# Block-sparse attention and a gated feed-forward: all heads visited whole, values in float32 by query half

## The chip, the cores and the metric

The kernel runs on one core of a Trainium2 chip. Its engines are TensorE (PE; PEld is its weight load), VectorE (DVE), ScalarE (ACT), GpSimd (POOL) and SyncE (SP), which issues most of the DMAs. The metric is the time of one execution on the device in microseconds (us), lower is better. Inputs and output lie in DRAM.

## The reference

There are 4 batches, 8 heads, 768 positions, head size 64, and blocks of 32 positions. The feed-forward has width 512 inside 2048.

```python
scores = scale * np.matmul(q, k.transpose(0, 1, 3, 2))      # per batch and head
mask = neighbours | first/last block row or column | 3 sampled blocks per block row
scores = np.where(mask, scores, -1000000000.0)
attn = softmax(scores)                                      # exp(scores - max) / (sum + 1e-9)
x = concat over heads of attn @ v                           # (4*768, 512)
h = x @ w_in
g = np.where(h >= 1, h, np.where(h <= -1, 0.0, (h + 1) ** 2 / 4))
out = g @ w_out
```

The mask is known only at run time, so the whole 768 x 768 score matrix is computed. The weights `moe_w_in` and `moe_w_out` arrive as 64-bit floats, which the kernel reads as pairs of 32-bit words and converts itself.

## The kernel before

**Numbers.** TensorE takes two kinds of operands here. A "rounded" one (fp32r) goes through in one record of a matmul; a float32 one in two. Where float32 accuracy is kept with rounded operands, a number is split into a rounded high part and the rounded rest, and two or three matmuls are added: scores are [q;k] high plus the cross terms (lines 411 and 412), the gated layers three products each (588 to 590, 624 to 626).

**A visit** (function `visit`) handles one head, or half of its queries. The queries and keys lie as columns (768 of them, in six tiles of 128, two halves of 384). Steps of a visit:

1. Maxima: 128 x 384 score tiles with the mask added through extra rows of q and k (line 356), reduced on VectorE (362), transposed on TensorE (375 or 379) and written with a minus sign into one more row of q (ScalarE, 384 or 387, or VectorE, 390).
2. Scores, transposed: keys on 128 partitions, 384 queries (409, or 411 and 412); the row of maxima takes part, so that ScalarE's exponential (416) follows at once.
3. Values: v times exponentials, accumulated over six key tiles (`values`).
4. Row sums of the exponentials, their reciprocal, and the product (x). For two heads at a time this makes 128 rows of x, which are split in high and rest (519, 524).

Before the change there are four forms. Batch 0 is visited twice: visits 0 to 7 take the first query half of each head with float32 scores straight from the loaded tiles (409); visits 8 to 15 the second half with split scores. Both multiply values in float32 at full width (445): v's 64 columns and 64 columns of ones, so that the row sums come out of the same matmul. Batch 1 (visits 16 to 23) multiplies values in float32 in two column groups of 64: even key tiles go to partitions 0 to 63 of the result, odd ones to 64 to 127 (448), and the two are added (457, 463). Batches 2 and 3 split the exponentials (ScalarE's cast, VectorE's subtraction at 424) and v, and take two rounded matmuls for each tile (451, 452). Outside batch 0, GpSimd adds the exponentials up (433), VectorE reduces them (479) and a small matmul finishes the row sums (485).

**The gated layers** (function `moe`) run for one half of a batch's rows at a time: 16 steps `fi` over the 2048 inner columns, each with 12 matmuls of 384 columns into `hp`, the gate on ScalarE and VectorE, and 9 matmuls of 512 columns into three accumulators `oa0` to `oa2`. Batch b's layers stand beside the attention of batch b+1; after the last batch they stand alone.

**Conversions** of the weights (`convert`) run on ScalarE and VectorE: one absolute value, four steps of 1024 columns (187 to 193) and two splits of 512 (200) for each of 8 pieces of w_in and 8 of w_out. The converted w_out is kept in DRAM and read again by each pass.

**What sets the order.** Every step is put in a list with a due time (`at(t, fn, ...)`, in units of one score tile, from tables of numbers at the end of the file) and emitted in that order; the scheduler of the tile framework then orders each engine's instructions by its own model of when operands are ready. Each engine executes its own order strictly. Score tiles share banks of PSUM: `pa` (three), and in batch 0 a ring of `oa0`, `oa1` and `hp` for the scores.

## Time and profile before

| What | us |
|---|---|
| Runs | 986.56, 989.36, 990.48 (median 989.36) |
| Profiled execution | 989.12 |
| Its span, first to last instruction | 987.3 |
| TensorE busy | 954.8 |
| VectorE busy | 691.8 |
| ScalarE busy | 636.5 |
| First scores | at 23.9 |
| First half of batch 0 | 23.9 to 98.2 |
| Second half of batch 0, with the start of the first gated pass | 98.2 to 205 |
| Batch 1, with the rest of batch 0's gated passes | 205 to 403 |
| Batches 2 and 3 | 403 to 845 |
| Gated passes alone | 845 to 987 |

How to read the profile: an engine's busy time is the union of its instructions' times. Matmuls overlap in their pipeline, so a matmul's own duration is longer than the time until the next one starts; the timeline by start times tells the rate. A float32 matmul appears as two records. Rows of the timeline give start, duration, engine, line, operation, output<-input and form, and in brackets the idle time before it with what ended it.

### The profile page before, as it was taken

The numbers are of one execution on the slowest core, as the hardware profiler recorded it, in microseconds if no ns is written. First come the engines' busy times: TensorE is split into PE (matmuls) and PEld (weight loads), VectorE is DVE, ScalarE is ACT, GpSimd is POOL, SyncE is SP. The second block draws the span as 40 slices with busy tenths as digits, with TensorE's granted clock in tenths as the row PEclk, the third lists the DMA queues.
The fourth block names the chain that finished last, engine by engine and source line by source line (L and its number), as shares of the span: only waits on it lengthen the run. The fifth ranks groups of instructions, "written<-read, shape, count | busy, mean of one in ns | idle before, by whom it ended". The sixth has DMA issues, their size and how long they took to land.

```text
span 987.3 us, 14438 instructions
## 1 busy us (share of the span) xinstructions
PE 954.8 (97%) x4770; PEld 811.0 (82%) x4770; DVE 691.8 (70%) x1268; ACT 636.5 (64%) x1286; POOL 263.1 (27%) x252
## 2 busy tenths in 40 slices
PE   2999999999999999999999999999999999999998
PEld 1656687877778777799999989999989999899997
DVE  3899976778756576888888897888888885422222
ACT  3698887665555554777767676767767676533433
POOL 1000000036444444333433343343433334000000
PEclk9999999999999999999999999999999999999999
DMA  6456764644555554655455444655545342433432
GB/s 181 135 183 221 216 200 159 180 138 136 153 168 152 143 154 133 178 155 171 140 142 176 139 137 144 185 158 153 157 132 168 115 126 86 155 128 128 160 128 96
DMA packets 55102, 150.83 MB, mean 153 GB/s; under 512 B 9414, under 2 KB 20310, under 8 KB 54004
## 3 DMA queue, kind: packets, MB, share of 16 engines
q1 hardware_dynamic: 54836, 149.42, 50.1%
q8 instruction: 38, 0.62, 0.3%
q10 hardware_dynamic: 192, 0.49, 0.1%
q14 instruction: 36, 0.29, 0.1%
HBM read 106.77 MB, written 14.80 MB: 123 GB/s over the span
## 4 chain that ended last, share of the span: by engine, by line
PE 86%; DMA 4%; ACT 4%; DVE 3%; issue 2%; SPq 0%; POOL 0%; ACTq 0%; DVEq 0%; POOLq 0%
PE oa L624 9%; PE oa L626 8%; PE oa L625 8%; PE hp L588 8%; PE hp L590 7%; PE hp L589 7%; PE pa L356 6%; PE pa L411 5%; PE pa L412 5%; PE po L445 4%; PE po L451 4%; PE po L452 3%; PE po L448 3%; PE oa L409 2%; PE oa L445 1%
## 5 line engine op out<-in xcount | busy, mean ns | idle before, releaser
L362 DVE TENSOR_REDUCE mc<-pa 128x1 f32<-128x384 f32 x384 | 204.9, 548 | 37.1 <-PE pa L356 34.0
L433 POOL TENSOR_TENSOR acc<-acc,pt 128x384 f32<-128x384 f32 x144 | 156.1, 1084 | 206.3 <-ACT pt L416 171.9
L416 ACT ACTIVATE pt<-pa 128x384 f32<-128x384 f32 x272 | 132.9, 489 | 59.0 <-PE pa L412 51.4
L588 PE MATMUL hp<-x,wi 128*128 128x384 f32 x448 | 156.7, 350 | 0.5 <-DVE r L603 0.5
L624 PE MATMUL oa<-w,gh 128*128 128x512 f32 x384 | 156.2, 407 | 0.3 <-ACT gh L215 0.3
L626 PE MATMUL oa<-w,gl 128*128 128x512 f32 x384 | 151.5, 394 | 0.0
L589 PE MATMUL hp<-x,wi 128*128 128x384 f32 x448 | 151.4, 338 | 0.0
L590 PE MATMUL hp<-x,wi 128*128 128x384 f32 x448 | 151.3, 338 | 0.0
L625 PE MATMUL oa<-w,gh 128*128 128x512 f32 x384 | 150.9, 393 | 0.0
L356 PE MATMUL pa<-KA,QA 88*128 88x384 f32 x384 | 143.0, 389 | 7.7 <-ACT QA L215 4.6
L424 DVE TENSOR_TENSOR pl<-pt,ph 128x384 fp32r<-128x384 f32 x192 | 125.7, 655 | 29.1 <-ACT ph L215 28.5
L215 ACT CAST ph<-pt 128x384 fp32r<-128x384 f32 x192 | 98.8, 515 | 69.8 <-PE po L451 66.9
L603 DVE SCALAR_TENSOR_TENSOR r<-r,hp 128x384 f32<-128x384 f32 x112 | 61.5, 549 | 86.0 <-ACT r L599 85.3
L411 PE MATMUL pa<-QA,KA 102*128 102x384 f32 (+1 forms) x336 | 116.3, 346 | 0.0
L412 PE MATMUL pa<-QB,KB 128*128 128x384 f32 x336 | 114.1, 340 | 0.0
L356 PEld LDWEIGHTS pa<-KA,QA 88*128 88x128 f32 x384 | 73.2, 192 | 34.8 <-DVE mc L362 7.4
L595 ACT ACTIVATE r<-hp,half_c 128x384 f32<-128x384 f32 x112 | 65.1, 582 | 52.8 <-PE hp L590 50.6
L614 DVE TENSOR_TENSOR gl<-r,gh 128x384 fp32r<-128x384 f32 x128 | 74.3, 580 | 27.4 <-ACT gh L215 26.8
L588 PEld LDWEIGHTS hp<-x,wi 128*128 128x128 f32 x448 | 84.5, 189 | 8.1 <-issue 1.8
L215 ACT CAST gh<-r 128x384 fp32r<-128x384 f32 x128 | 65.6, 513 | 32.8 <-DVE r L603 32.2
L589 PEld LDWEIGHTS hp<-x,wi 128*128 128x128 f32 x448 | 84.4, 188 | 2.6
L626 PEld LDWEIGHTS oa<-w,gl 128*128 128x128 f32 x384 | 72.1, 188 | 17.2
(125 smaller groups left out, 1676.1 us busy)
## 6 DMA issues: line engine op xcount, KB each, us to landing
w<-wo_dram SPq DMA_DIRECT2D x112, 512.0 KB
qk<-in_qk_t_dram SPq DMA_DIRECT2D x24, 384.0 KB
raw<-in_moe_w_in_dram SPq DMA_DIRECT2D x8, 1024.0 KB
raw<-in_moe_w_out_dram SPq DMA_DIRECT2D x16, 512.0 KB
wo_dram<-w SPq DMA_DIRECT2D x16, 512.0 KB
lv<-in_v_dram SPq DMA_DIRECT2D x40, 192.0 KB
den<-s SPq DMA_DIRECT2D x64, 96.0 KB
out_dram<-o SPq DMA_DIRECT2D x7, 768.0 KB
```

The source lines that it names most:

```text
L215: eng.copy(out=dst, in_=src)
L356: nc.tensor.matmul(out=pm[:, 0:HALF], lhsT=QAi[0:KM, t * 128:(t + 1) * 128], rhs=KAi[0:KM, kh * HALF:(kh + 1) * HALF], start=True, stop=True)
L362: nc.vector.reduce_max(out=st["mc"][:, t - t0, kh:kh + 1], in_=st.pop(("pm", t, kh))[:, 0:HALF], axis=AX.X)
L411: nc.tensor.matmul(out=ps[:, 0:HALF], lhsT=KAi[0:k, ks], rhs=QAi[0:k, cs], start=True, stop=False)
L412: nc.tensor.matmul(out=ps[:, 0:HALF], lhsT=st["KB"][:, ks], rhs=st["QB"][:, cs], start=False, stop=True)
L433: nc.gpsimd.tensor_tensor(out=st["acc", hf], in0=prev, in1=st["p", hf, c], op=ALU.add)
L588: nc.tensor.matmul(out=hv, lhsT=wi[:, j, 0, fs], rhs=x[:, 0], start=(j == 0), stop=False)
L589: nc.tensor.matmul(out=hv, lhsT=wi[:, j, 0, fs], rhs=x[:, 1], start=False, stop=False)
L590: nc.tensor.matmul(out=hv, lhsT=wi[:, j, 1, fs], rhs=x[:, 0], start=False, stop=(j == NP - 1))
L624: nc.tensor.matmul(out=o, lhsT=gh[:, ts], rhs=w[:, 0], start=(fi == 0), stop=False)
L625: nc.tensor.matmul(out=o, lhsT=gh[:, ts], rhs=w[:, 1], start=False, stop=False)
L626: nc.tensor.matmul(out=o, lhsT=gl[:, ts], rhs=w[:, 0], start=False, stop=(fi == NF - 1))
```

## The change

All 32 heads are visited once, whole, in one form. q and k are loaded together (768 columns), rounded on ScalarE, and copied to their places by DMA; the scores are always two rounded matmuls (now lines 323 and 324). Values are always float32 in two column groups of 64, but the groups now are the two query halves (345): all 12 matmuls of a head belong to one step, and the results are copied without an addition (352). v needs no split and no ones any more, the exponentials aren't split. Maxima are always transposed to one row, six transposes a head (302).

In batch 0 the row sums come from TensorE: 12 float32 matmuls a head with a stationary tile of 32 columns of ones, dealt out to four column groups of 32 (368). The sums go through DRAM to be turned (377, 383). In the other batches GpSimd adds the exponentials up as before, for the two halves one after the other, and the reduction and the finishing matmul are done once for a pair of heads instead of once for each half.

Batch 0's gated passes now begin after batch 0's attention. They are split by `fi`: first half 0 with steps 0 to 7, then half 1 with all 16, then half 0 with steps 8 to 15. The partial output of the first goes to DRAM and is read back and added in the third (537). Conversions are cut so that each piece serves one quarter of w_in's columns for two row tiles, and the tables of due times are new.

Core of the diff:

```diff
+    def mask_half(hf, eng):
+        cs = slice(hf * HALF, (hf + 1) * HALF)
+        pm = psa.tile([128, 512], F32, name="pa")
+        nc.tensor.matmul(out=pm[0:NB, 0:HALF], lhsT=early["mb"][M], rhs=KAt[0][64:KM, cs], start=True, stop=True)
+        rounded(eng, QA[0][64:KM, cs], pm[0:NB, 0:HALF])
...
+    def visit(n, b, h, pst):
 
         j, e = divmod(h, 2)
+        n0 = PER * n
         wide = n < H
-        raw = n in RAW
-        whole = n in WHOLE
-        tiled = n in TILED
-        row = n in ROW
-        G = {**P, **PW} if wide else {**P, **PX} if n < 2 * H else {**P, **PA} if n < 3 * H else P
-        o0, o1 = (L, R) if e == 0 else (R, L)
+        G = {**P, **PW} if wide else {**P, **PA} if n < 2 * H else P
+        o0 = (L, R)[e]
         QAi, KAi = QA[n % SETS], KAt[n % SETS]
...
+        at(-99 if n == 0 else n0 - G["qs"] - G["ld"], load_qk)
+        at(n0 - G["qs"] - 0.4, hi)
+        at(n0 - G["qs"] + 0.2, hi_one)
+        at(n0 - G["qs"] + 0.4, lo)
+        at(n0 - G["qs"] + 1.3, hi_two)
+        at(n0 - G["qs"] + 1.6, lo_two)
...
-            ps = st["ps", c] = bank(wide)
-            k = 97 if row else KA
-            if raw:
-                nc.tensor.matmul(out=ps[:, 0:HALF], lhsT=KF[n % RAWS][0:k, ks], rhs=QF[n % RAWS][0:k], start=True, stop=True)
-                return
-            nc.tensor.matmul(out=ps[:, 0:HALF], lhsT=KAi[0:k, ks], rhs=QAi[0:k, cs], start=True, stop=False)
+            ps = st["ps", hf, c] = bank(wide)
+            nc.tensor.matmul(out=ps[:, 0:HALF], lhsT=KAi[0:97, ks], rhs=QAi[0:97, cs], start=True, stop=False)
...
-        def p_hi(hf, c):
-            ph = st["ph", c] = pp.tile([128, HALF], F32R, name="ph")
-            rounded(nc.scalar, ph, st["p", hf, c])
-
-        def p_lo(hf, c):
-            pl = st["pl", c] = pp.tile([128, HALF], F32R, name="pl")
-            nc.vector.tensor_tensor(out=pl, in0=st["p", hf, c], in1=f(st["ph", c]), op=ALU.subtract)
+            p = st["p", hf, c] = pp.tile([128, HALF], F32, name="pt")
+            nc.scalar.activation(out=p, in_=st.pop(("ps", hf, c))[:, 0:HALF], func=AF.Exp, scale=SCALE)
...
-            if whole:
-                nc.tensor.matmul(out=po, lhsT=st["vn"][:, c], rhs=st["p", hf, c], start=(c == 0), stop=(c == T - 1))
-                return
-            if tiled:
-                nc.tensor.matmul(out=st["po", hf][R if c % 2 else L, 0:HALF], lhsT=st["lv"][:, c], rhs=st["p", hf, c],
-                                 start=(c < 2), stop=(c >= T - 2))
-                return
-            nc.tensor.matmul(out=po, lhsT=st["vn"][:, c], rhs=st["ph", c], start=(c == 0), stop=False)
-            nc.tensor.matmul(out=po, lhsT=st["vn"][:, c], rhs=st["pl", c], start=False, stop=(c == T - 1))
...
+        def values(g):
+            after(("V", n, g), *[("V", n, k) for k in range(g)])
+            if g == 0:
+                st["po"] = psc.tile([128, DM], F32, name="oa2") if wide and n % 2 else pso.tile([128, 512], F32, name="po")
+            for c in range(g * VG, (g + 1) * VG):
+                for hf in range(2):
+                    nc.tensor.matmul(out=st["po"][(L, R)[hf], 0:HALF], lhsT=st["lv"][:, c], rhs=st["p", hf, c],
+                                     start=(c == 0), stop=(c == T - 1))
+
+        def o_copy(hf):
+            after(("x", b, j, hf, e), ("V", n, T // VG - 1))
+            if e == 0 and hf == 0:
+                pst["xun"] = pr.tile([128, 2, HALF], F32, name="xun", bufs=2)
+            nc.scalar.copy(out=pst["xun"][o0, hf], in_=st["po"][(L, R)[hf], 0:HALF])
...
+        def p_tot():
+            after(("tot", n), ("V", n, T // VG - 1))
+            pd = st["tot"] = bank(wide)
+            for c in range(T):
+                for hf in range(2):
+                    k = 2 * (c % 2) + hf
+                    nc.tensor.matmul(out=pd[k * 32:(k + 1) * 32, 0:HALF], lhsT=ones, rhs=st["p", hf, c],
+                                     start=(c < 2), stop=(c >= T - 2))
+
+        def p_row():
+            after(("ps", b, j, e), ("tot", n))
             if e == 0:
...
+                pst["s1"] = dr.tile([2, 2, 2, HALF], F32, name="s1", bufs=2)
+            a = ac.tile([128, 2, HALF], F32, name="acc")[:, 0]
+            nc.scalar.copy(out=a, in_=st["tot"][:, 0:HALF])
+            Q_S1.dma_start(out=pst["s1"][e].rearrange("q f c -> (q f) c"), in_=a[0:128:32])
+
+        def r_in():
+            after(("in", b, j), ("ps", b, j, 0), ("ps", b, j, 1))
+            t = pst["rt"] = pr.tile([48, 2, 32], F32, name="rt")
+            for k in range(2):
+                Q_T.dma_start(out=t[k * 24:(k + 1) * 24], in_=pst["s1"][k].rearrange("q f (a j) -> (f a) q j", j=32))
+
+        def r_den():
+            after(("r", b, j), ("in", b, j))
+            t = pst["r"] = pr.tile([48, 32], F32, name="rc", bufs=2)
+            nc.vector.scalar_tensor_tensor(out=t, in0=pst["rt"][:, 0], scalar=1e-9, in1=pst["rt"][:, 1], op0=ALU.add, op1=ALU.add)
...
+        if wide:
+            at(u + 0.01, p_tot)
+            at(u + G["al"], p_row)
             if e:
...
+        def o_tile():
+            g["out"] = op.tile([128, 3, DM], F32, name="o")
+            if not first:
+                after(("back", b, hf), ("part", b, hf))
+                Q_OUT.dma_start(out=g["out"], in_=part)
+
         def o_copy(t):
-            after(("oc", b, hf, t), *[("l2", b, hf, k, t) for k in range(NF)])
-            if t == 0:
-                g["out"] = op.tile([128, 3, DM], F32, name="o")
-            if end and t == 1:
...
+    full = tuple(range(NF))
+    low, high = full[:NF // 2], full[NF // 2:]
+    t = PER * H + D0
+    for hf, fis, new in ((0, low, low), (1, full, high), (0, high, ())):
+        moe(t, STEP0, 0, hf, fis, new)
+        t += STEP0 * len(fis)
+    for k in range(2, 2 * B):
+        moe(PER * H * (1 + k / 2) + DELAY, PER * H / 2 / NF, k // 2, k % 2, full)
...
-RAW = tuple(range(8))
-WHOLE = tuple(range(16))
-TILED = tuple(range(16, 24))
-LV, VG, VD = 3, 6, 0.0
-ROW = tuple(range(24))
-KMOVE = 0
...
+LV, PT, VG, XT = 3, 14, 6, 10
+STEP0 = 2.598
+D0 = 10.127
```

How the order moves, at the places that the prediction uses. TensorE in batch 0, in a visit's second part, before (409 float32 scores, 356 maxima of the next visit, 445 values at full width):

```order
L409 MATMUL oa_521<-QB,KB 128x384
L356 MATMUL pa<-KA_116,QA_114 128x384
L445 MATMUL oa_509<-pl,vn 128x384
L409 MATMUL oa_531<-QB,KB 128x384
L356 MATMUL pa<-KA_116,QA_114 128x384 x2
L445 MATMUL oa_509<-pt,vn 128x384
L409 MATMUL hp<-QB,KB 128x384
```

The same place now (323 and 324 scores, 285 maxima of the next head, 345 values in column groups, 368 row sums, 302 transposes):

```order
L345 MATMUL oa_1172<-pt,lv 64x384 x2
L285 MATMUL pa<-KA_112,QA_110 128x384 x2
L323 MATMUL oa_1152<-QA_111,KA_113 128x384
L285 MATMUL pa<-KA_112,QA_110 128x384
L324 MATMUL oa_1152<-QB,KB 128x384
L345 MATMUL oa_1172<-pt,lv 64x384 x2
L285 MATMUL pa<-KA_112,QA_110 128x384 x2
L345 MATMUL oa_1172<-pt,lv 64x384 x2
L285 MATMUL pa<-KA_112,QA_110 128x384
L345 MATMUL oa_1172<-pt,lv 64x384
L368 MATMUL oa_1185<-pt,ones 32x384 x9
L302 MATMUL pa<-idr,mr 1x128 x6
```

Single float32 matmuls at full width among the maxima have become short groups of one or two matmuls in column groups, and a block of row sums stands ahead of the transposes. Over batch 0 the 96 value matmuls (345) stand in 56 such groups and the 96 row-sum matmuls (368) in 25.

TensorE in the later batches, before (451 and 452 values, 624 to 626 the second gated layer, 411 scores):

```order
L626 MATMUL oa_5785<-w,gl 128x512
L451 MATMUL po<-ph,vn 128x384
L452 MATMUL po<-pl,vn 128x384
L624 MATMUL oa_5803<-w,gh 128x512
L625 MATMUL oa_5803<-w,gh 128x512
L626 MATMUL oa_5803<-w,gl 128x512
L411 MATMUL pa<-QA_114,KA_116 128x384
```

And now (523 gated layer, 393 finishing matmul of the row sums, 345 values, 323 and 324 scores, 487 gated layer):

```order
L523 MATMUL oa_6587<-w,gl 128x512
L393 MATMUL pa<-sel,PS_114 64x32
L345 MATMUL po<-pt,lv 64x384 x12
L323 MATMUL pa<-QA_111,KA_113 128x384
L324 MATMUL pa<-QB,KB 128x384
L487 MATMUL hp<-x,wi 128x384
```

Twelve pairs of rounded value matmuls, spread over a head, have become one closed group of twelve.

VectorE at the start, before (362 reductions of the first maxima, 188 and 189 conversion of w_in, 367 the maxima's last step):

```order
L362 TENSOR_REDUCE mc<-pa 128x1 x6
L188 TENSOR_SCALAR cva<-cva 128x1024
L367 TENSOR_TENSOR mr<-mc 128x3
L189 TENSOR_SCALAR cva<-cva 128x1024
L362 TENSOR_REDUCE mc<-pa 128x1 x2
```

And now (258 the rest of q and k, 220 the mask's row, 291 reductions, 296 the maxima's last step, 197 conversion):

```order
L258 TENSOR_TENSOR qk<-qk,qkh 128x768
L220 CAST QA_110<-pa 24x384
L291 TENSOR_REDUCE mc<-pa 128x1 x12
L296 TENSOR_TENSOR mr<-mc 128x6
L197 TENSOR_SCALAR cva<-cva 128x1024
```

The first conversion step has moved behind the first head's maxima, which are twelve instead of six.

More of the change, by code (lines that the diff above doesn't have):

```diff
@@ L394, in visit, with max_turn @@
-        jobs = [(t, kh) for t in tiles for kh in range(2)]
+            nc.vector.tensor_tensor(out=mr, in0=st["mc"][:, :, 0], in1=st["mc"][:, :, 1], op=ALU.max)
+        def max_turn(hf):
+            after(("turn", n, hf), ("col", n))
+            pm = st["pr", hf] = bank(wide, "m")
+            for t in range(TH):
+                nc.tensor.transpose(out=pm[0:1, t * 128:(t + 1) * 128].bitcast(F32R),
+                                    in_=st["mr"][:, hf * TH + t:hf * TH + t + 1], identity=idr)
@@ new lines, in sums, with dens, recip @@
+        def sums():
+            after(("sums", b, j), ("ps", b, j, 0), ("ps", b, j, 1))
+            pd = st["pd"] = bank(wide)
+            nc.tensor.matmul(out=pd[0:64, 0:32], lhsT=pst["ps"], rhs=sel, start=True, stop=True)
+        def dens():
+            after(("r", b, j), ("sums", b, j))
+            t = pst["r"] = pr.tile([48, 32], F32, name="rc", bufs=2)
+            nc.vector.tensor_single_scalar(out=t, in_=st["pd"][0:48, 0:32], scalar=1e-9, op=ALU.add)
+        def recip():
+            after(("rr", b, j), ("r", b, j))
+            nc.vector.reciprocal(out=pst["r"], in_=pst["r"])
+            pst["den"] = pr.tile([128, S], F32, name="den", bufs=1)
+            s2 = dr.tile([2, S], F32, name="s2", bufs=2)
+            Q_S2.dma_start(out=s2.rearrange("e (a b) -> (e a) b", b=32), in_=pst["r"])
+            for k in range(2):
+                Q_DEN.dma_start(out=pst["den"][k * 64:(k + 1) * 64], in_=s2[k:k + 1].to_broadcast([64, S]))
@@ L523, in x_lo @@
             x = xt[b, j, hf]
[L524 to L528 removed]
+            nc.vector.tensor_tensor(out=x[:, 1], in0=pst["xun"][:, hf], in1=f(x[:, 0]), op=ALU.subtract)
+        for c in range(T):
+            for hf in range(2):
+                s = n0 + 2 * c + hf
                 at(s, scores, hf, c)
                 at(s + G["ex"], expo, hf, c)
[L531 to L534 removed]
+                if not wide:
@@ new lines, in visit @@
+        for hf in range(2):
+            at(u + G["ot"], o_copy, hf)
+        if wide:
+            at(u + 0.01, p_tot)
+            at(u + G["al"], p_row)
+            if e:
+                y = u + G["su"]
+                at(y, r_in)
+                at(y + G["de"], r_den)
+        else:
+            at(n0 + 2 * T - 1 + G["al"] + G["ps"], acc_sum)
+        if e and not wide:
+            y = u + G["su"] + (PER if h < H - 1 else G["al"])
+            at(y, sums)
+            at(y + G["de"], dens)
@@ L562, in body, with moe @@
+        if e:
+            at(y + G["re"], recip)
+            y += G["r2"] + G["re"]
+            at(y + G["xm"], x_mul)
+            for hf in range(2):
+                at(y + G["xh"] + 0.01 * hf, x_hi, hf)
+                at(y + G["xl"] + 0.01 * hf, x_lo, hf)
     wo_dram = dr.tile([NF, 128, 2 * DM], F32R, name="wo_dram")
-    def moe(t0, p, b, hf, first):
+    part = dr.tile([128, 3, DM], F32, name="part")
+    def moe(t0, p, b, hf, fis, new=()):
         g = {}
-        G = {**P, **PM} if first else P
+        G = {**P, **PM} if new else P
+        first, final = fis[0] == 0, fis[-1] == NF - 1
```

438 lines of the change are left out of this document (126 added, 312 removed).

## The prediction

> **What bounds the kernel now.** I read part 1 of the page first, then the stages by windows, then the order in time of TensorE alone.
>
> ```profile
> PE 954.8 (97%) x4770; PEld 811.0 (82%) x4770; DVE 691.8 (70%) x1268; ACT 636.5 (64%) x1286; POOL 263.1 (27%) x252
> 23.90:98.20 74.30, 73.72 (x252) 45.20 (x251) 67.21 (x114) 61.19 (x119) 0.00 (x0) 1.00 0.56 179
> 98.20:205.00 106.80, 104.21 (x476) 81.03 (x475) 85.78 (x147) 83.33 (x164) 1.25 (x1) 1.00 0.63 191
> 205.00:403.00 198.00, 193.69 (x1021) 151.07 (x1019) 130.01 (x236) 112.10 (x229) 87.78 (x81) 1.00 0.50 146
> 403.00:624.00 221.00, 219.92 (x1160) 203.56 (x1161) 184.78 (x348) 156.96 (x328) 85.06 (x80) 1.00 0.52 152
> 624.00:845.00 221.00, 220.11 (x1161) 203.37 (x1161) 177.37 (x334) 156.05 (x328) 84.30 (x79) 1.00 0.48 141
> 845.00:987.30 142.30, 138.09 (x693) 123.93 (x691) 39.41 (x72) 57.99 (x109) 0.00 (x0) 1.00 0.39 133
> ```
>
> A window row gives length, then busy time of PE, PEld, DVE, ACT, POOL, granted clock, DMA share and GB/s. TensorE fills every stage after the first scores; the others have room. So I count what TensorE has to issue. A busy matmul overlaps its neighbour, so a price is the distance from one start to the next:
>
> ```profile
> 318.21 0.34 PE L411 MATMUL pa<-QA,KA 97*128 97x384 f32 x1
> 318.39 0.34 PE L412 MATMUL pa<-QB,KB 128*128 128x384 f32 x1
> 318.56 0.33 PE L588 MATMUL hp<-x,wi 128*128 128x384 f32 x1
> ...
> 319.09 0.52 PE L375 MATMUL pa<-idr,mr 128*1 128x128 f32 x6
> 319.45 0.39 PE L588 MATMUL hp<-x,wi 128*128 128x384 f32 x1
> ...
> 321.43 0.39 PE L624 MATMUL oa<-w,gh 128*128 128x512 f32 x1
> 321.66 0.40 PE L625 MATMUL oa<-w,gh 128*128 128x512 f32 x1
> ```
>
> A rounded (fp32r) matmul of 384 columns costs 0.175 us, one of 512 columns 0.233, a transpose of a maximum 0.36/6 = 0.06. Float32 at full width:
>
> ```profile
> 36.86 0.81 PE L445 MATMUL po<-pt,vn 128*128 128x384 f32 x2
> 37.50 0.81 PE L409 MATMUL hp<-QB,KB 97*128 97x384 f32 x2
> 37.85 0.81 PE L356 MATMUL pa<-KA,QA 88*128 88x384 f32 x2
> 38.50 0.81 PE L445 MATMUL po<-ph,vn 128*128 128x384 f32 x2
> ```
>
> One float32 matmul is two records. From 36.86 to 38.50 lie one value matmul, one float32 score and two maxima: (1.64 - 0.35)/2 = 0.645 each, with nothing lost at the changes. Float32 in column groups, first a closed group of six, then scattered:
>
> ```profile
> 313.11 0.33 PE L356 MATMUL pa<-KA,QA 88*128 88x384 f32 x1
> 313.38 0.54 PE L448 MATMUL po<-pt,lv 128*64 128x384 f32 x1
> 313.38 0.54 PE L448 MATMUL po<-ph,lv 128*64 128x384 f32 x1
> 313.75 0.49 PE L448 MATMUL po<-pt,lv 128*64 128x384 f32 x1
> ...
> 314.07 0.49 PE L448 MATMUL po<-pl,lv 128*64 128x384 f32 x1
> ...
> 315.46 0.44 PE L356 MATMUL pa<-KA,QA 88*128 88x384 f32 x1
> 315.74 0.40 PE L624 MATMUL oa<-w,gh 128*128 128x512 f32 x1
> ```
> ```profile
> 217.54 0.33 PE L356 MATMUL pa<-KA,QA 88*128 88x384 f32 x1
> 217.81 0.54 PE L448 MATMUL po<-pt,lv 128*64 128x384 f32 x1
> 217.82 0.54 PE L448 MATMUL po<-ph,lv 128*64 128x384 f32 x1
> 218.60 0.44 PE L356 MATMUL pa<-KA,QA 88*128 88x384 f32 x1
> 218.98 0.86 PE L448 MATMUL po<-pl,lv 128*64 128x384 f32 x2
> 219.77 0.44 PE L356 MATMUL pa<-KA,QA 88*128 88x384 f32 x1
> ```
>
> The two groups start together, and a record follows every 0.32 us: a pair of matmuls costs one slot of 0.64. But the group of three slots takes 313.11 to 315.74, less two rounded matmuls of 0.175: 2.28, where 3 x 0.64 = 1.92. So each **run** (column-group matmuls with none at full width between) pays 0.36 for getting in and out. A lone matmul with no partner (218.60 to 219.77, less one maximum) costs 0.99: as much as a pair, and 1.5 times the full-width 0.645. This is what the change multiplies.
>
> I check the prices on the kernel before. Batch 0, first half: 96 float32 (61.9), 48 maxima (8.4), 24 transposes (1.4) = 71.7 of the 74.3. From 98.2 to 403: 48 float32 (31.0), 816 rounded of 384 (142.8), 279 of 512 (65.0), 16 runs (36.5), 72 transposes (4.3) = 280 of 304.8. From 403 on: 2112 of 384 (369.6), 873 of 512 (203.4), 16 transposes (1) = 574 of 584.3. So 3, 25 and 10 us are waits and the tail.
>
> **The change part by part.** Counts are from TensorE's order in the changed program.
>
> Start: before, the first scores wait for a conversion that stands among VectorE's first maxima:
>
> ```profile
> 13.97 2.88 DVE L362 TENSOR_REDUCE mc<-pa 128x1 f32<-128x384 f32 x6 [2.81 <-PE pa L356]
> 20.26 1.12 ACT L187 ACTIVATE cva<-raw 128x1024 f32<-128x1024 f32 x1 [4.80 <-DMA raw<-in_moe_w_in_dram]
> 22.03 0.15 DVE L367 TENSOR_TENSOR mr<-mc 128x3 fp32r<-128x3 f32 x1
> 23.86 2.76 PE L409 MATMUL oa<-QB,KB 97*128 97x384 f32 x4
> ```
>
> Now the first conversion stands behind twelve maxima and their transposes. Against that stand twelve reductions instead of six (another 2.9) and one hop more: q and k are loaded whole, rounded on ScalarE and copied into place by DMA. A hop of a few KB takes 2.48 in the row below; bigger copies more. Maxima from about 13.5, ending 19.3, row written and scores at 21. Bounds: 18 (the load no later) to 26 (the hop's queue fills with the w_in loads issued behind it).
>
> ```profile
> 342.75 2.48 DMA s<-rc
> ```
>
> Batch 0 (eight heads whole, until the last row-sum matmul): 91 maxima and 192 rounded score matmuls, 283 x 0.175 = 49.5; 42 transposes 2.5; 96 value matmuls in 56 runs and 62 slots, 56 x 0.36 + 62 x 0.64 = 59.8; the 96 new row-sum matmuls with ones in 25 runs. The last have four groups of 32 columns, which no row shows. If four share a slot, 34 slots: 25 x 0.36 + 34 x 0.64 = 30.8; if two, 56 slots: 44.8; if none, 70.4. I take four, since two groups in the rows cost each other nothing. Sum 142.6. Waits: 6, against 3 in the old first stage, because no MoE matmul is left to fill gaps here. VectorE doesn't bound it: 96 maxima at 0.548 are 52.6, and all else it did in the old first stage (67.2 - 48 x 0.548) is 41. ScalarE's 96 exponentials at 0.489 are 47, all else 38. So about 149, where the old stages spent 74.3 on the first half and, on the second half's share of the next window, 48 float32 (31), 144 rounded (25.2), 1.4 and some waits, say 60. The split scores save 48 x (0.645 - 0.35) = 14; the row sums and the runs take back 31 + 20.
>
> ```profile
> L362 DVE TENSOR_REDUCE mc<-pa 128x1 f32<-128x384 f32 x384 | 204.9, 548 | 37.1 <-PE pa L356 34.0
> L416 ACT ACTIVATE pt<-pa 128x384 f32<-128x384 f32 x272 | 132.9, 489 | 59.0 <-PE pa L412 51.4
> L424 DVE TENSOR_TENSOR pl<-pt,ph 128x384 fp32r<-128x384 f32 x192 | 125.7, 655 | 29.1 <-ACT ph L215 28.5
> ```
>
> On the drain: the Trainium skill (TensorEngine Tiling (Array Packing), Key Properties) says that changing the tiling mode, not just the tile, drains TensorE. By it the step from value runs (64 wide) straight to row-sum runs (32 wide) pays as well, which no row here shows; I priced it as any run, and without that price the sum is some 3 us lower.
>
> Batch 1 with batch 0's gated passes: 677 rounded of 384 (118.5), 288 of 512 (67.1), 54 transposes (3.2), 18 value runs in 53 slots (40.4), row sums 1: 230, plus 8 for waits (half of what the old stage had beyond the prices, as the scattered full-width values are gone). Splitting the passes by f moves loads of w and one partial output through DRAM; those and the converted w_out share the DMA queues, at 0.50 busy in that stage, so nothing on the path.
>
> Batches 2 and 3: per head 24 rounded value matmuls (4.2) become one run of six slots (0.36 + 3.84 = 4.2). Six transposes take the place of one: 16 x 0.3 = 4.8. Row sums half as often, -2; the extra runs at one head's scatter, +2. So 584.3 + 5 = 589. The 125.7 us of L424 and ScalarE's casts before it vanish, but those engines already idle at least 36 of 221 us there, TensorE 1: worth nothing on the path. It would be worth something only if TensorE waited for them, which the 219.92 busy of 221.00 excludes to within 1 us per batch.
>
> **Sum.** 21 + 149 + 238 + 589 = 997 for the span, against 987.3; the profiled execution took 989.1, its span and 1.8 around it, and the median of the runs is 989.4. So 997 + 2, rounded: **999 us**. Bounds add up from 18 to 26 at the start, 25 + 56 runs at nothing (-29) or row sums two to a slot (+14) or alone (+40), and waits 0 to 25.
>
> **Rivals.**
> 1. *The runs cost nothing more* (faster). If the scattered runs of batch 0 stand where TensorE would wait for exponentials anyway, their 81 x 0.36 = 29 us are covered: 970. For it: the scores go three banks ahead of ScalarE at 0.489 each, while a rounded pair needs 0.35. Against: both other engines' sums, 94 and 85, lie far below 149, and the scattered rows at 215 to 220 paid the price in the midst of other work. It decides once the mean price of a run falls under 0.18.
> 2. *Row sums don't share four ways* (slower). For it: only two groups ever ran together here. Two to a slot: 1013; one after the other: 1039. It decides if starts of L368 don't come in fours.
> 3. *All cancels* (no change). Start at 18, no waits in batch 0 and half of them in batch 1: 999 - 3 - 6 - 4 = 986. For it: the old first stage had 3 us of waits in 74.
> 4. *The last pair's row sums come late.* They go through DRAM twice (a copy, two hops in, two hops out, 2.5 to 3 each), then three vector steps: about 15 us before the first gated pass can use that pair. TensorE's order holds about 20 us of batch 1's work ahead of it. If the hops take 4, some 2 to 5 us: within the main case.
>
> **Numbers.** Main case 0.50 (988 to 1012), rival 1 0.22, rival 2 0.10, rival 3 0.18. Two runs of this kernel can be told apart from about 0.5%, that is 984.4 to 994.3 for no change. The main case gives 0.08 of it to no change, rival 3 gives 0.12 there, 0.03 to faster and 0.03 to slower: faster 0.25, same 0.20, slower 0.55. The range leaves out the lower half of rival 1 and the worst of rival 2: 970 to 1018. The main case's own range is 988 to 1012.
>
> **What would show it.** Right: the last L368 near 170; L345 alone among L323 at about 1.0 us; in batches 2 and 3 still 221 us and TensorE above 99% while VectorE falls by 60 us a batch or more. Rows of L368 starting in fours 0.01 apart and 0.32 between show the row sums' price. Wrong: the last L368 near 140 (rival 1), gaps on TensorE in batch 1 left by VectorE's conversions, or batches 2 and 3 shorter than 215, which would mean that the stage waited for something that busy time hides.

## The result and the profile after

The changed kernel takes **998.4 us** (median of four runs, 997.67 to 999.98) against 988.86 for the kernel before in the same session: ratio 1.010, 95% interval 1.0075 to 1.0126. It is slower by about 1%, and the forecast was 999. The profiled execution has a span of 995.9. First the page's line of busy times, then the stages by windows from the first scores on, cut at the end of batch 0's row sums, at the end of batch 1's attention, between batches 2 and 3, and at the start of the lone gated passes.

```profile
PE 971.9 (98%) x5018; PEld 764.5 (77%) x5018; DVE 540.6 (54%) x918; ACT 527.9 (53%) x1043; POOL 257.5 (26%) x253
```
```profile
19.10:167.30 148.20, 145.87 (x710) 69.75 (x710) 93.95 (x160) 80.52 (x166) 0.00 (x0) 0.99 0.58 164
167.30:408.00 240.70, 235.59 (x1220) 190.97 (x1219) 174.33 (x271) 140.95 (x279) 87.60 (x80) 1.00 0.59 182
408.00:624.00 216.00, 215.75 (x1157) 180.49 (x1156) 114.34 (x200) 119.74 (x237) 83.27 (x80) 1.00 0.53 150
624.00:845.50 221.50, 221.06 (x1194) 188.43 (x1190) 107.53 (x189) 122.35 (x242) 82.77 (x80) 1.00 0.49 142
845.50:995.90 150.40, 146.27 (x727) 130.77 (x725) 40.84 (x74) 60.85 (x114) 0.00 (x0) 1.00 0.40 131
```

VectorE lost 151 us of work and ScalarE 109; TensorE gained 17, and the span grew by 8.6. The first scores come 4.8 us earlier, at 19.1. From there to the end of batch 1's stage it is 389 us, where the kernel before took 379 (23.9 to 403). The rest, 588 us against 584, differs by little, and how it is divided between its last rows depends on where I cut.

The first scores, a pause in batch 0, a piece of its middle and its end, in TensorE's order of time:

```profile
19.14 0.69 PE L323 MATMUL oa<-QA,KA 97*128 97x384 f32 x1 [0.25 <-ACT QA L307]
19.62 0.52 PE L324 MATMUL oa<-QB,KB 128*128 128x384 f32 x1
19.94 0.52 PE L323 MATMUL hp<-QA,KA 97*128 97x384 f32 x1
...
42.47 0.44 PE L323 MATMUL oa<-QA,KA 97*128 97x384 f32 x1 [1.58 <-ACT QA L307]
...
43.63 0.52 PE L323 MATMUL oa<-QA,KA 97*128 97x384 f32 x1
43.95 0.52 PE L324 MATMUL oa<-QB,KB 128*128 128x384 f32 x1
...
124.87 0.87 PE L345 MATMUL oa<-pt,lv 128*64 128x384 f32 x4
125.67 0.44 PE L285 MATMUL pa<-KA,QA 88*128 88x384 f32 x1
126.04 0.86 PE L345 MATMUL oa<-pt,lv 128*64 128x384 f32 x2
126.83 2.12 PE L368 MATMUL oa<-pt,ones 128*32 128x384 f32 x18
128.88 0.52 PE L302 MATMUL pa<-idr,mr 128*1 128x128 f32 x6
...
166.47 0.84 PE L368 MATMUL oa<-pt,ones 128*32 128x384 f32 x4
```

The 18 records from 126.83 are nine row-sum matmuls. They take 2.05 us: three slots of 0.64 and the edge. So four do share a slot, as I took it. The Trainium skill (TensorEngine Tiling (Array Packing), Available Configurations) lists four tiles for 128 rows by 32 columns. The trace agrees. A pair of value matmuls (four records at 124.87) and a lone one (two at 126.04) each take 0.8 to the next instruction, and more is lost behind them. Leaving the 64-column groups for 32-column ones (126.04 to 126.83) costs the same 0.79 to the next start as leaving them for a full-width matmul (0.80).

The rounded score matmuls from 19.62 and from 43.63 on start 0.32 us apart, where the price is 0.175. From 42.9 to 46.3 the trace has the granted clock at 0.50. Before 25.8 it has no record of the clock (the column then reads 1.00), but the pitch of 0.32 is the same.

The forecast's total held. Whether its reasons held is another question; by the experiments only some of them did.

### The profile page after: what moved, and what is told of

It is laid out like the page before. It is cut to its first block, busy times and chain, and to the rows that moved or that the text cites. A ratio compares the mean times of both kernels' runs of the same rounds, so it can differ in the third digit from the quotient of the medians.

```text
span 995.9 us, 13899 instructions
## 1 busy us (share of the span) xinstructions
PE 971.9 (98%) x5018; PEld 764.5 (77%) x5018; DVE 540.6 (54%) x918; ACT 527.9 (53%) x1043; POOL 257.5 (26%) x253
## 4 chain that ended last, share of the span: by engine, by line
PE 88%; DVE 5%; DMA 4%; ACT 2%; issue 1%; SPq 0%; ACTq 0%
PE po L345 12%; PE oa L521 8%; PE oa L522 8%; PE oa L523 8%; PE hp L487 7%; PE hp L488 7%; PE hp L489 7%; PE pa L285 7%; PE pa L323 5%; PE pa L324 5%; PE oa L345 3%; DMA qk<-in_qk_t_dram 2%; DVE mc L291 2%; PE oa L323 2%; PE oa L368 1%; PE oa L324 1%
## 5 line engine op out<-in xcount | busy, mean ns | idle before, releaser
L337 POOL TENSOR_TENSOR acc<-acc,pt 128x384 f32<-128x384 f32 x192 | 201.2, 1049 | 217.4 <-ACT pt L328 214.5
L328 ACT ACTIVATE pt<-pa 128x384 f32<-128x384 f32 x288 | 140.5, 491 | 129.8 <-PE pa L324 121.6
L521 PE MATMUL oa<-w,gh 128*128 128x512 f32 x384 | 151.5, 395 | 0.3 <-ACT gh L224 0.3
L522 PE MATMUL oa<-w,gh 128*128 128x512 f32 x384 | 151.4, 394 | 0.0
L337 POOL TENSOR_TENSOR acc<-pt 128x384 f32<-128x384 f32 x48 | 52.6, 1097 | 360.0 <-ACT pt L328 196.8
L345 PE MATMUL po<-pt,lv 128*64 128x384 f32 x672 | 133.0, 496 | 0.0
L285 PE MATMUL pa<-KA,QA 88*128 88x384 f32 x384 | 128.8, 364 | 4.1 <-DMA QA<-qkh 2.2
L513 DVE TENSOR_TENSOR gl<-r,gh 128x384 fp32r<-128x384 f32 x128 | 89.7, 700 | 50.1 <-ACT gh L224 49.2
L323 PE MATMUL pa<-QA,KA 97*128 97x384 f32 x288 | 101.8, 353 | 1.7 <-DVE mc L291 0.7
L285 PEld LDWEIGHTS pa<-KA,QA 88*128 88x128 f32 x384 | 71.3, 192 | 38.8 <-DVE mc L291 27.6
L324 PE MATMUL pa<-QB,KB 128*128 128x384 f32 x288 | 97.7, 339 | 0.0
L345 PEld LDWEIGHTS po<-pt,lv 128*64 128x64 f32 x672 | 55.3, 137 | 47.6 <-issue 40.1
```

What stands on the lines that cost most here:

```text
L285: nc.tensor.matmul(out=pm[:, 0:HALF], lhsT=QAi[0:KM, t * 128:(t + 1) * 128], rhs=KAi[0:KM, kh * HALF:(kh + 1) * HALF], start=True, stop=True)
L323: nc.tensor.matmul(out=ps[:, 0:HALF], lhsT=KAi[0:97, ks], rhs=QAi[0:97, cs], start=True, stop=False)
L324: nc.tensor.matmul(out=ps[:, 0:HALF], lhsT=st["KB"][:, ks], rhs=st["QB"][:, cs], start=False, stop=True)
L337: nc.gpsimd.tensor_tensor(out=st["acc"][:, hf], in0=prev, in1=st["p", hf, c], op=ALU.add)
L345: nc.tensor.matmul(out=st["po"][(L, R)[hf], 0:HALF], lhsT=st["lv"][:, c], rhs=st["p", hf, c], start=(c == 0), stop=(c == T - 1))
L521: nc.tensor.matmul(out=o, lhsT=gh[:, ts], rhs=w[:, 0], start=(fi == fis[0]), stop=False)
```

## The experiments

TensorE's sum for a stage is counted below as in the prediction, from the order of its instructions and the prices there. "Kernel before" is always the one run beside the experiment. The changed kernel's ratio to it is 1.010.

### What a run costs: six pairs in place of one group

```diff
+        VG = 1 if n >= 2 * H else 6
         for g in range(T // VG):
             u = n0 + 2 * (g + 1) * VG - 1 + G["lag"]
```

> Only batches 2 and 3 change: each head's twelve value products are issued as six pairs among the scores and the gated layers, in place of one group of twelve. By the order of the instructions that makes 99 runs and 99 slots there in place of 22 runs and 97 slots; batches 0 and 1 stay as they are. My theory (0.36 us a run): 77 runs more, 28 us, and 2 slots, 1 us: about 1027. Rival A (a price per slot, not per run): 2 slots more, about 1000. Rival B (a run's loss at its edges is hidden by the loading of the next weights): 998.

Measured: **1026.9 us**, ratio 1.0415 (1.0386 to 1.0443). That is 28.5 us more than the changed kernel by the medians, 27.6 by the spans, 31 by the ratios; 29 were expected. One pair in its trace, in TensorE's order of time:

```profile
503.10 0.40 PE L524 MATMUL oa<-w,gl 128*128 128x512 f32 x1
503.43 0.87 PE L345 MATMUL po<-pt,lv 128*64 128x384 f32 x4
504.22 0.44 PE L323 MATMUL pa<-QA,KA 97*128 97x384 f32 x1
504.50 0.34 PE L324 MATMUL pa<-QB,KB 128*128 128x384 f32 x1
```

From 503.10 to 504.50 are 1.40 us. Less the two full-width matmuls (0.233 and 0.175) the pair takes 0.99: one slot of 0.64 and 0.35 for the run. The loss lies on both sides: 0.10 before, 0.15 in the pair's own distance, 0.10 behind. In a stage that TensorE bounds, the price of a run is right, and it adds up.

Where a value run in batch 0 goes straight into a row-sum run, the pair is cheaper than two runs. From 126.04 to 128.88 above, four slots take 2.84 us, 0.28 more than 4 x 0.64. With the 0.10 on each outer side the two runs lose 0.48 together, where the prediction counted 0.72. There are seven such places.

### Less work for TensorE in batch 0: row sums by GpSimd

```diff
-                if not wide:
-                    at(s + G["ps"], p_sum, hf, c)
+                at(s + G["ps"], p_sum, hf, c)
...
-            at(u + 0.01, p_tot)
-            at(u + G["al"], p_row)
...
+        at(n0 + 2 * T - 1 + G["al"] + G["ps"], acc_sum)
```

> Batch 0's row sums go back to GpSimd's additions, as in the other batches; the value products stay in column groups. My theory: the 96 row sums in 25 runs and 34 slots, 30 us of TensorE's time, were all on the path: about 968 (966 to 975, since GpSimd's 80 additions of 1.1 us, 88 us, fit within the 118 us left of the stage). Rival (row sums filled pauses in which TensorE would have waited for exponentials): 990 to 998. Rival (GpSimd holds the exponentials' tiles longer and TensorE waits for it): 980 or more.

Measured: **1004.8 us**, ratio 1.0187 (1.0157 to 1.0217). TensorE has 30 us less to do and the kernel is 6 us slower than the changed one. The theory that every microsecond off TensorE counts falls here. Windows of three stretches of batch 0, then rows from the end of the third head: VectorE's, then TensorE's.

```profile
19.00:60.00 41.00, 36.19 (x138) 19.97 (x138) 33.24 (x46) 21.97 (x44) 22.71 (x20) 0.92 0.52 152
60.00:104.00 44.00, 36.12 (x136) 19.57 (x135) 33.92 (x53) 22.69 (x47) 24.26 (x20) 0.85 0.60 174
104.00:147.00 43.00, 36.86 (x135) 19.92 (x134) 27.82 (x43) 18.57 (x39) 22.58 (x20) 0.82 0.57 158
```
```profile
75.22 0.98 DVE L358 TRANSPOSE_TENSOR_REDUCE PS<-acc 128x24 f32<-128x768 f32 x1 [4.44 <-POOL acc L337]
```
```profile
76.69 4.40 PE L285 MATMUL pa<-KA,QA 88*128 88x384 f32 x9 [3.61 <-DVE mc L291]
...
84.00 0.52 PE L324 MATMUL oa<-QB,KB 128*128 128x384 f32 x1
84.32 0.52 PE L323 MATMUL hp<-QA,KA 97*128 97x384 f32 x1
```

VectorE's queue holds the transposing reduction of a finished head ahead of the next head's twelve maxima. The reduction waits 4.4 us for GpSimd's last addition, and TensorE, which has nothing else, waits for the maxima. Behind that wait the granted clock is no longer 1.00, and the score matmuls from 84.00 on follow each other by 0.32 us in place of 0.175. So there are three candidates: the wait in the queue, something that slows VectorE, and the clock.

What TensorE lost can be estimated. In the three stretches it waits 18.6 us by the view of waits, against 2.5 in the changed kernel's batch 0. The missing clock is 0.08 x 41 + 0.15 x 44 + 0.18 x 43, at most 18 us, against 2 there. That is 16 us more of each, up to 32 of the 37 us by which the run lies above the 968 of my theory.

### The clock: keep TensorE busy with work that nobody needs

Against the version with GpSimd's sums:

```diff
         at(n0 + 2 * T - 1 + G["al"] + G["ps"], acc_sum)
+        if wide:
+            at(u + 0.01, p_tot)
```

> The version with GpSimd's row sums (1004.8), and beside it the 96 matmuls with ones of the changed kernel, whose result nobody reads: some 30 us more for TensorE in batch 0, 142 us in place of 111. If the falling granted clock (0.82 to 0.92 in that stage) is what made the shorter TensorE work no faster: the clock goes back to 0.97 or more and the time is 1000 to 1012, although TensorE does 30 us more. If TensorE's work adds up whatever the clock: 1025 or more.

Measured: **1011.1 us**, ratio 1.0236 (1.0202 to 1.0269). Thirty microseconds more for TensorE cost 6 by the medians (5 by the ratios). Windows as above:

```profile
19.00:60.00 41.00, 38.09 (x176) 18.93 (x179) 33.97 (x47) 22.26 (x46) 23.59 (x20) 1.00 0.52 152
60.00:104.00 44.00, 41.18 (x201) 19.21 (x194) 34.59 (x53) 24.41 (x49) 23.77 (x21) 0.96 0.69 181
104.00:147.00 43.00, 37.52 (x181) 17.99 (x181) 24.49 (x42) 17.38 (x36) 20.78 (x20) 0.93 0.56 163
```

The clock rose to between 0.93 and 1.00; 0.97 or more was expected. So in the version with GpSimd's sums TensorE's time in batch 0 is set from elsewhere: its matmuls run slowly, or useless ones stand between them, and the end moves little.

### GpSimd beside VectorE, and the version at full width

The next version gives the values of batch 0 back to full width, with 64 columns of ones beside v, so that one matmul makes values and row sums. GpSimd gets nothing.

```diff
-    ones = cst.tile([128, 32], F32, name="ones")
+    VW = [f(wst.tile([128, 2, DM], F32R, name="w").rearrange("p a d -> p (a d)"))[:, 0:T * 128].rearrange("p (t d) -> p t d", t=T) for i in range(2)]
...
+        nc.gpsimd.memset(VW[0][:, :, 64:128], 1.0)
+        nc.gpsimd.memset(VW[1][:, :, 0:64], 1.0)
...
+                    if wide:
+                        nc.tensor.matmul(out=st[("po", "po2")[hf]][:, 0:HALF], lhsT=VW[e][:, c], rhs=st["p", hf, c],
+                                         start=(c == 0), stop=(c == T - 1))
+                        continue
...
-            at(u + 0.01, p_tot)
```

> Batch 0's values go back to full width: each head's v stands beside 64 columns of ones, so the 96 value matmuls also give the row sums, and the 96 matmuls with ones go. GpSimd gets nothing. By the order of the instructions TensorE's sum for batch 0 falls from 141 to 114 us. My first theory (TensorE's sum sets batch 0, every microsecond off it counts): 971. My new theory after the run with GpSimd's sums (batch 0 is held nearly as tightly by VectorE's maxima at the head boundaries, and where TensorE waits there its granted clock falls, so that its next matmuls cost up to double): 985 to 1000, with a granted clock under 0.95 in batch 0. If 975 or less, what cost the time there was GpSimd beside VectorE alone.

Measured: **979.7 us**, ratio 0.9906 (0.9875 to 0.9938): faster than both kernels. It is 18.7 us below the changed one, between my two theories, and the clock stayed at 1.00. A matmul of values and sums costs 0.65 between neighbours at full width (TensorE's order of time):

```profile
100.52 0.81 PE L348 MATMUL po<-pt,w 128*128 128x384 f32 x2
101.17 0.81 PE L348 MATMUL oa<-pt,w 128*128 128x384 f32 x2
...
148.45 0.81 PE L348 MATMUL oa<-pt,w 128*128 128x384 f32 x2
```

Batch 0's last one stands at 148.45, where the changed kernel's last row sum stands at 166.47: the 18 us are all there. Of the remaining 8 to 9 of the 27, about half went into waits: those that the view of waits gives for TensorE in batch 0 grew from 2.5 to 7.1 us. The other half isn't traced.

On this version GpSimd was then given 80 additions that nothing reads. Against the full-width version:

```diff
+    junk = cst.tile([128, HALF], F32, name="junk")
+    nc.gpsimd.memset(junk, 0.0)
...
+            if wide and c:
+                tc.keep_in_program_order(nc.gpsimd.tensor_tensor(out=junk, in0=junk, in1=junk, op=ALU.add))
```

> The full-width version (979.7), with 80 useless GpSimd additions of 128x384 that wait for nothing and run one after the other from the start, some 88 us, until about the fifth head of batch 0. TensorE's and VectorE's own work is unchanged. If GpSimd beside VectorE is what cost the time when GpSimd made the row sums: VectorE's conversions get longer (L202's 1.22 us to 1.45 or more) while the additions run, TensorE waits for maxima there, and the time is 990 to 1005. If it was the order of VectorE's queue (the transposing reductions that wait for GpSimd) or the tiles held longer: 978 to 984.

Measured: **995.6 us**, ratio 1.0083 (1.0052 to 1.0114): 16 us lost by additions that wait for nothing and hold nothing. Windows of the full-width version, then of the one with additions, then its VectorE groups from 19.3 to 101 (busy time, mean ns):

```profile
19.30:60.00 40.70, 36.33 (x145) 26.66 (x146) 30.05 (x48) 26.24 (x53) 0.00 (x0) 1.00 0.66 186
60.00:101.00 41.00, 40.18 (x182) 29.89 (x181) 34.90 (x63) 27.06 (x58) 0.00 (x0) 1.00 0.70 203
```
```profile
19.30:60.00 40.70, 34.70 (x129) 24.98 (x129) 32.12 (x42) 22.00 (x44) 37.88 (x37) 0.92 0.58 163
60.00:101.00 41.00, 35.32 (x132) 25.86 (x131) 35.84 (x47) 21.27 (x47) 37.01 (x35) 0.83 0.55 148
101.00:149.00 48.00, 46.78 (x200) 33.82 (x199) 29.73 (x56) 27.89 (x60) 0.00 (x0) 1.00 0.70 183
```
```profile
L294 DVE TENSOR_REDUCE mc<-pa 128x1 f32<-128x384 f32 x48 | 24.5, 551 | 7.1 <-PE pa L288 7.1
L203 DVE SCALAR_TENSOR_TENSOR cva<-raw,cva 128x1024 int32<-128x1024 int32 x5 | 8.4, 1674 | 0.1
L299 DVE TENSOR_TENSOR mr<-mc 128x6 fp32r<-128x6 f32 x4 | 3.1, 784 | 0.0
```

In the full-width version without the additions the second and third of these groups are, over the same time:

```profile
L201 DVE SCALAR_TENSOR_TENSOR cva<-raw,cva 128x1024 int32<-128x1024 int32 x6 | 7.3, 1223 | 0.1
L297 DVE TENSOR_TENSOR mr<-mc 128x6 fp32r<-128x6 f32 x5 | 0.8, 160 | 0.0
```

While GpSimd adds, VectorE's instructions with two inputs from SBUF take 0.3 to 0.6 us longer (0.45 and 0.62 in these rows), even the one of six columns; the reductions from PSUM do not (551 ns). In 19.3 to 101, 48 maxima are done in place of 60, TensorE issues 66 records fewer and its clock falls. After 101, when GpSimd is through, TensorE's clock is 1.00 again. The Trainium skill (SBUF — State Buffer, Who interferes with whom) states this: a VectorE instruction with two SBUF inputs contends with a GpSimd instruction that reads SBUF, a reduction does not. The trace agrees on both. It is not only those: the conversion steps with one input (TENSOR_SCALAR, 1024 columns) took 0.95 to 1.01 us in place of 0.69.

So GpSimd beside VectorE costs time by itself. How much of the loss with GpSimd's row sums comes from it isn't shown. There GpSimd was busy 23 to 24 us of each stretch, where the useless additions kept it busy for 37 to 38; the two-input conversion steps took 1.45 to 1.55 us in place of 1.22, the step of six columns took 0.13, and VectorE had the transposing reductions and the wait in its queue on top. The shares weren't separated.

### Closed groups in batch 0

Two attempts to buy back the price of the 81 runs. In the first the program order is kept strictly until a due time of 97:

```diff
+    early_plan = [x for x in plan if x[0] < MANUAL]
+    with tc.manual_schedule():
+        for _, fn, args in early_plan:
+            fn(*args)
-    for _, fn, args in plan:
+    for _, fn, args in plan[len(early_plan):]:
...
+MANUAL = 97
```

> Batch 0 runs in the order of the table of due times, so the twelve value products of a head stand in one closed run and its twelve row sums in another: 16 runs in place of 81, 72 slots in place of 96, the same 192 matmuls. My theory (each run costs 0.36 us over its slots of 0.64): TensorE's sum for batch 0 falls from 141 to 105 us, so about 962 if nothing new waits, up to 972 if the exponentials of the next head wait for free tiles while a head's products run. Rival A (a slot costs 0.94 whatever stands around it, the 90.6 us over 96 slots): 24 slots fewer, 22.6 us, about 976. Rival B (batch 0 is paced by ScalarE's exponentials and VectorE's maxima, TensorE is only busy at a slower pitch): no change, 998.

Measured: **1079.5 us**, ratio 1.0937 (1.0913 to 1.0961), far from all three. The edit fixes the order of every engine and queue, not of TensorE's groups alone. TensorE waits 46 us in batch 0, in eight waits, for copies of q and k that are issued late (the one below at 120.98, behind the row sums' hop at 120.04). Its rows around this wait:

```profile
124.23 0.98 PE L285 MATMUL pa<-KA,QA 88*128 88x384 f32 x2 [5.19 <-DMA QA<-qkh]
125.01 0.52 PE L323 MATMUL hp<-QA,KA 97*128 97x384 f32 x1
125.33 0.52 PE L324 MATMUL hp<-QB,KB 128*128 128x384 f32 x1
...
128.21 0.34 PE L323 MATMUL hp<-QA,KA 97*128 97x384 f32 x1
128.38 0.34 PE L324 MATMUL hp<-QB,KB 128*128 128x384 f32 x1
```

As a test of the runs it is void. But it shows the clock plainly: after a pause of 5.2 us matmuls follow each other by 0.32 us (granted clock 0.50), and 4.0 us later by 0.175 again (1.00). The Trainium skill (TensorE: Matmul & The Clock Gate, HAM oscillation — how this bites in real kernels) says that a pause over about 3.4 us halves the clock. The trace agrees here and behind the 3.61 us pause above. But in this case the length of one pause doesn't decide alone. The changed kernel had its half clock from 42.9 behind a pause of 1.58 us, the version with GpSimd's sums from 100.9 and from 121.4 (0.50 in both) at pauses of 1.58 and 1.15 us, while a pause of 2.67 us in the full-width version left it at 1.00. What else decides wasn't found.

In the second only the order within a head's values is turned round:

```diff
-            for c in range(g * VG, (g + 1) * VG):
-                for hf in range(2):
+            cs = range(T - 1, -1, -1) if wide else range(T)
+            for c in cs:
+                for hf in ((1, 0) if wide else (0, 1)):
...
-                                     start=(c == 0), stop=(c == T - 1))
+                                     start=(c == cs[0]), stop=(c == cs[-1]))
```

> Only the order of batch 0's value matmuls within a head is turned round, the last exponential's first, so that a head's values cannot start before its last exponential and stand closer together: by the order of the instructions 42 runs and 49 slots in place of 56 and 62; the row sums stay at 25 runs. Price of a run right and TensorE the only bound: 13 us less, 985. New theory (batch 0 is held by the head boundaries too, where TensorE now waits for exponentials with nothing to fill in, at a falling clock): 998 or more, up to 1020.

Measured: **996.1 us**, ratio 1.0070 (1.0045 to 1.0094). Its interval overlaps that of the changed kernel, so a gain of 13 us is excluded and one of 2 or 3 is possible. It lies just under the 998 of the new theory. Fourteen runs fewer buy next to nothing. In batch 0 TensorE's waits grow from 2.5 to 9.7 us, for the row of maxima and the exponentials above all, and its clock is at 0.50 for 14 us where it was for 3, worth up to 5 us by estimate.

### VectorE's relief in batches 2 and 3

```diff
             nc.scalar.activation(out=p, in_=st.pop(("ps", hf, c))[:, 0:HALF], func=AF.Exp, scale=SCALE)
+            if n >= 2 * H:
+                y = pp.tile([128, HALF], F32, name="ph", bufs=1)
+                nc.vector.tensor_tensor(out=y, in0=p, in1=p, op=ALU.subtract)
```

> In batches 2 and 3 VectorE gets a useless subtraction of 128x384 for each of the 192 exponentials (0.655 us each, 126 us in all), which nothing reads. That gives VectorE back the work that the change took from it, in about the same place. My theory: VectorE's relief was worth nothing, since TensorE bounds these stages: 998 to 1000 (the order of the instructions has two slots more). Rival (the relief was worth part of its 126 us, and something else in the change took that back): 1005 to 1040.

Measured: **1031.3 us**, ratio 1.0446 (1.0424 to 1.0468). My theory said 998 to 1000; it falls. VectorE waits 64 us inside its queue for exponentials, so the next run took that wait away:

```diff
+    junk = cst.tile([128, 1, HALF], F32, name="junk")
+    nc.gpsimd.memset(junk, 0.0)
...
+            if n >= 2 * H:
+                tc.keep_in_program_order(nc.vector.tensor_tensor(out=junk[:, 0], in0=junk[:, 0], in1=junk[:, 0], op=ALU.subtract))
```

> The same 192 useless subtractions of 128x384 on VectorE in batches 2 and 3 as in the run before, but of a tile of its own that waits for nothing, at the same places of the program. The run before took 33 us more; its trace shows VectorE waiting 64 us for exponentials inside its queue, with the maxima behind. If the wait in the queue made the cost: 998 to 1006. If the work itself did (VectorE's 126 us, and GpSimd and VectorE slowing each other): 1020 to 1035.

Measured: **1028.6 us**, ratio 1.0404 (1.0378 to 1.0430). The wait wasn't it. The waits of TensorE there, and rows of VectorE, GpSimd and TensorE at the end of one head's maxima:

```profile
PE pa L304 <- DVE mr L298: 13.5, 13, 1.2
```
```profile
481.60 0.95 DVE L298 TENSOR_TENSOR mr<-mc 128x6 fp32r<-128x6 f32 x1
```
```profile
480.13 2.39 POOL L341 TENSOR_TENSOR acc<-acc,pt 128x384 f32<-128x384 f32 x2 [1.57 <-ACT pt L330]
```
```profile
482.69 0.52 PE L304 MATMUL pa<-idr,mr 128*1 128x128 f32 x6 [1.11 <-DVE mr L298]
```

The last step of the maxima, six columns, takes 0.95 us here beside GpSimd's additions (0.90 on average, against 0.22 in the changed kernel) and comes late for the transposes, in 13 of 16 heads. How late it may come is set by the distance from a head's last maximum to its transposes. Here are the two TensorE rows of the kernel before, then of the changed one:

```profile
500.14 0.34 PE L356 MATMUL pa<-KA,QA 88*128 88x384 f32 x1
...
504.36 0.22 PE L379 MATMUL pa<-idr,mr 128*6 128x128 f32 x1
```
```profile
502.98 0.34 PE L285 MATMUL pa<-KA,QA 88*128 88x384 f32 x1
...
505.98 0.52 PE L302 MATMUL pa<-idr,mr 128*1 128x128 f32 x6
```

The kernel before leaves 4.2 us, and 3.9 in every other head; the changed one leaves 3.0. The third run keeps the useless work and moves the maxima ahead. Of the long line `P` only the three entries that change are given; batch 1 keeps its old ones through `PA`.

```diff
-P = {... 'qs': 8.321, ... 'm0': 7.7, ... 'mc': 2.3, ...}
+P = {... 'qs': 9.821, ... 'm0': 9.2, ... 'mc': 3.8, ...}
-PA = {}
+PA = {'m0': 7.7, 'mc': 2.3, 'qs': 8.321}
```

> The 192 useless subtractions that wait for nothing, as in the last run (1028.6), but the maxima of batches 2 and 3 (and the rounding and copies of q and k ahead of them) are due 1.5 units earlier, so that TensorE has 5.4 to 6.0 us of other work between a head's last maximum and its transposes in place of 3.0. If VectorE's work costs time because the twelve maxima then end too late for the transposes (13 waits of about 1.1 us, 13.5 us in all, in the last run's trace): those waits go, 1015 or less, and down to 1000 if the small waits for free banks go with them. If the work as such costs the time, wherever the maxima stand: 1025 to 1030.

Measured: **1014.9 us**, ratio 1.0272 (1.0245 to 1.0299). The view of TensorE's waits has no row for the transposes any more; its longest row is 2.8 us, for the gate.

So of the 30 us that VectorE's old load costs in the changed kernel, 14 went when the maxima moved ahead. The other 16 are small pauses, most of them before and behind maxima, where a bank seems to come free late; their full cause stays open. TensorE's busy time hides most of them. This is the window of batches 2 and 3:

```profile
408.00:863.70 455.70, 449.48 (x2345) 366.05 (x2345) 356.83 (x580) 240.84 (x478) 187.39 (x160) 1.00 0.49 140
```

TensorE counts as busy for 98.6% of it, and yet by the profiled executions these stages are 18 us longer than the changed kernel's 437.5 (216.0 and 221.5). The load is not free in this plan, though VectorE is idle for half of these stages without it and for a fifth with it.

### The passes over all of f at once

```diff
-    for hf, fis, new in ((0, low, low), (1, full, high), (0, high, ())):
+    for hf, fis, new in ((0, full, full), (1, full, ())):
...
-            convert(PER * H + D0 + (u - 4) * CSTEP - CONV + (STEP0 * NF / 2 if u > 3 else 0), ...
+            convert(PER * H + D0 + (u - 4) * CSTEP - CONV, ...
```

> The first gated passes are whole again: pass 0 over all of f, with every conversion in it, then pass 1; no partial output goes through DRAM. TensorE's sum changes by 2 us at most. My theory: the split spreads the conversions over two passes and without it the first pass waits for VectorE's conversions (16 blocks of about 6 us against a pass of some 42 us of its own plan): 1005 to 1025, with TensorE's waits for converted weights in batch 1. Rival (conversions were hidden either way): 996 to 1000.

Measured: **1001.0 us**, ratio 1.0127 (1.0096 to 1.0157), an interval that overlaps that of the changed kernel. I expected 1005 or more. The conversions were nearly hidden either way, and the split is worth about 3 us, if anything.

## Why the prediction was right, and where its reasons were not

**The sum.** Predicted and measured: first scores 21 and 19.1; batch 0 from there 149 and 148 (last row sum by 167; "near 170" was said); batch 1 238 and 241; the rest 589 and 588. Each term lies within 3 us. That is more than luck: the runs' price was confirmed alone (29 predicted, 28.5 measured), and four row sums to a slot are seen in the rows. Inside batch 0's term there is some luck. Of its 6 us of waits 2.5 came as waits. The rest is slow matmuls, which the sum didn't have: 0.32 us apart from the first scores to about 25.8, and half clock for 3.4 us from 42.9. These 10 us at half speed are worth some 5 by estimate. Against it stand the seven places where a value run meets a row-sum run, counted some 2 us too high.

**Rival 1 (the runs cost nothing more) is wrong as it was put,** since a run did cost 0.36 in the measured stage. But its core, that batch 0 has other work close behind TensorE's, is half right. Taking a fifth of TensorE's work away there brought a loss of 6 us with GpSimd's sums and a gain of 19 at full width, and a tenth of it (the last exponential first) a gain of about 2; never the full amount. **Rival 2** (row sums not shared) falls by the trace. **Rival 3** (all cancels) falls by the result; its early start did come. **Rival 4** (late row sums) was no matter: the view of TensorE's waits in batch 1 has no row for x.

**The step that doesn't carry further is "VectorE doesn't bound it".** I compared sums of busy time (94 us of VectorE against 149) and took the difference for reserve. What matters is when a head's last maximum is ready, and there the reserve was small. The changed kernel itself stays on the right side: TensorE's waits in batch 0 are 2.5 us, less than the 6 I gave. But with less work TensorE waits at the heads' ends, and its clock falls there as well. By my sum the version with GpSimd's sums would take 968; it took 1005.

**"Worth nothing on the path" was right in its number and wrong in its reason.** The old 221 us a batch became 216 and 221.5, as said. But the reason (VectorE idles, so its load does not matter) would make the reverse edit free, and it cost 30 us. Nor does a busy share of 219.92 in 221.00 exclude losses "to within 1 us per batch", as I wrote: the last of the three runs lost 18 us of span in these stages at 98.6%. The changed plan leaves the maxima 0.9 to 1.2 us less lead than the old one, and it needs VectorE's idle time at that place. What else makes the old load cost little in the old plan and 30 us in the new one is open: more lead than in either still left 16.

**Where the gain went.** The split scores save 14 us by the prediction's prices and the earlier start 5, and 260 us of lighter work on the other two engines shorten no stage beyond the forecast, which gave them nothing. The scattered column groups and the separate row sums take it back: at full width, with everything else of the change kept, batch 0 ends 18 us earlier and the kernel takes 979.7.

## What to carry to other kernels

Each run of column-group matmuls between full-width ones pays about 0.36 us for getting in and out, more than half of a full-width float32 matmul of 384 columns; use column groups in closed runs, or take full width and let the spare columns do something (ones, for the row sums). A sum over one engine forecasts well what added work costs where that engine has no pauses (29 us forecast, 28.5 measured; with pauses 30 us of work cost 6), and badly what removed work brings: before counting on a gain, look at which engine's chain ends next at the same place, and whether pauses there would lower TensorE's clock (one of 1.58 us did here). A busy share near 100% doesn't show that an engine loses nothing. Work that is moved to GpSimd isn't free for VectorE: count VectorE's instructions on SBUF that stand beside it, those with two inputs first.

## What the runs showed of the hardware that I had not expected

- Beside GpSimd's additions an instruction of VectorE on six columns took 0.78 to 0.95 us in place of 0.16, the conversion step of 1024 columns with two inputs 1.67 in place of 1.22 and that with one 0.95 to 1.01 in place of 0.69, while reductions from PSUM kept their 0.55.
- 30 us of added matmuls cost 6 us in a stage with pauses, and the granted clock rose with them: from 0.82 to 0.85 in two stretches of batch 0 to 0.93 to 0.96.
- After a pause of 5.2 us score matmuls came every 0.32 us for 4.0 us, then every 0.175 again. A pause of 1.58 us was followed by half clock for 3.4 us, one of 2.67 us in another version was not.
- A change from 64-column to 32-column groups took as long as one to full width to the next start (0.79 against 0.80 us), and without the 0.10 that a run loses on each side next to full-width matmuls.
